# Merging an attention stream and a projection stream on one core: values one head behind, four shared PSUM banks, column tiles, gate products apart from the convolution

## The chip, the core and the metric

The kernel runs on one core of a Trainium2 chip. The metric is device time in microseconds (us). The names used below are those of the profile: PE is the matrix engine, PEld its weight loads, DVE the vector engine, ACT the scalar engine, POOL the general-purpose engine, SP the queue that issues most DMAs. PSUM is PE's output memory; the kernel's pools divide it into eight banks, and a tile of up to 512 fp32 columns takes one.

## The reference, cut to what matters

Two stages. The first is attention with a hash mask, over 4 batches of 8 heads (768 positions, 64 columns a head). The second is a gated long convolution on the attention's output, 512 columns wide.

```python
q_bits = (q @ proj > 0); k_bits = (k @ proj > 0)      # 6 bits each
mask = bucket(q_bits)[:, None] == bucket(k_bits)[None, :]
attn = softmax(where(mask, q @ k.T / 8, -1e9))         # per head
x = attn @ v                                           # heads side by side: 768 x 512
x1, x2, x3 = split(x @ w_proj, 3)
x2_conv = irfft(rfft(x2) * rfft(filter))               # along the sequence
out = (x1 * x2_conv * x3) @ w_out
```

## The kernel before

Heads are processed in pairs, 16 pairs in all, four pairs to a batch. For each pair the kernel transposes q and k on PE (`tps`), copies them out of PSUM with a scale on DVE (`tz`), multiplies by the hash matrix in fp32 on PE (`zps`), and makes +-0.5 bits on DVE that become extra rows of the operands (`pr_q`, `pr_k`). Scores (`stp`) go to exp on ACT (`pt`), and values (`pv`) follow. ACT copies one half of `pv` to `S`, and DVE adds it to the other half, which gives `T`. The normalisation goes through memory: row sums leave by DMA (`lt`), a reciprocal (`rl`), out to DRAM (`rdr`) and back, spread over the partitions (`R`). `U` multiplies by R, and `xh` and `xl` are its fp16 high and low halves. The projection of a batch then has x2 (`x2a`, `x2b`, `x2c`), a transform by matrices (`fdft`, with `u` and `z` on DVE), its inverse (`ida`, `idrq`, giving `cv`), x1 and x3 (`x`, 384 columns), and `wout`.

```python
psS = tile_pool(bufs=2)      # scores: 2 banks each
psV = tile_pool(bufs=1)      # values: 2 banks
psW = tile_pool(bufs=2)      # all the rest: 1 bank each

def prep(g, which):          # ... transposes into tps, tz ...
    for hf in range(2):
        zps = psW.tile([70, HALF], ...)
        nc.tensor.matmul(zps, projpad, tz[:, cs])       # fp32, 70 weight columns
        nc.vector.tensor_scalar(row[(which, 0)][64:70, cs], zps[64:70, :], ...)
        nc.vector.tensor_scalar(row[(which, 1)][0:6, cs], zps[0:6, :], ...)

def head(g, par, vpr, S, T):
    for jt in range(NCH):                               # 6 chunks
        stp = psS.tile([P, SEQ], ...)                   # two matmuls, 512 + 256
        nc.scalar.activation(pt[:, 0:SEQ], stp, AF.Exp, ...)
    pv = psV.tile([P, SEQ + 1], ...)
    for jt in range(NCH): ...                           # two matmuls each, 512 + 257
    nc.scalar.copy(S[rows, :], pv[HD:P, :])
    nc.vector.scalar_tensor_tensor(T[rows, :], in0=S[rows, :], ..., in1=pv[0:HD, :])

def pair(g):                 # ... both heads ...
    nc.sync.dma_start(lt[:, par, :], S[r0 : r0 + 1, 0:SEQ])
    # ... rl = 1 / (lt + eps); rdr <- rl; R <- rdr ...
    nc.vector.scalar_tensor_tensor(U, in0=T[:, 0:SEQ], scalar=vsd, op0=ALU.add, in1=R, op1=ALU.mult)
    # ... xh = fp16(U) on DVE, xl = U - xh on POOL ...

for b in range(1, NBAT):
    for pr in range(NPAIR):
        pair(b * NPAIR + pr); prep_pair(b * NPAIR + pr + 2)
    phase_b(b - 1, fbp)      # the whole projection of the batch before
phase_b(NBAT - 1, fbp)
```

A recording layer takes these instructions and orders them on each engine before the kernel runs, by its own model of when each is ready. At run time each engine's order is fixed.

The softmax here doesn't subtract the row's maximum and nothing guards it: scores larger than these inputs give would overflow.

Of the kernel before, what the change touches and what calls it, by code (L numbers as in the profile page):

```python
# [15 lines left out]
P = 128  # L16
SEQ = 768
# [69 lines left out]
def kernel(  # L87
# [35 lines left out]

    cp = ctx.enter_context(tc.tile_pool(name="consts", bufs=1))
    drp = ctx.enter_context(tc.tile_pool(name="drs", bufs=2, space=bass.MemoryType.DRAM))
    psS = ctx.enter_context(tc.tile_pool(name="psS", bufs=2, space=bass.MemoryType.PSUM))
    psV = ctx.enter_context(tc.tile_pool(name="psV", bufs=1, space=bass.MemoryType.PSUM))
    psW = ctx.enter_context(tc.tile_pool(name="psW", bufs=2, space=bass.MemoryType.PSUM))
    natp = ctx.enter_context(tc.tile_pool(name="nat", bufs=5))
    tzp = ctx.enter_context(tc.tile_pool(name="tz", bufs=2))  # L130
# [4 lines left out]
    nc.sync.dma_start(cst_sb, cst_d.ap())  # L135
    ident = cst_sb[:, 0:P]
    mask = cst_sb[:, P : P + 1]
    projpad = cp.tile([P, 70], FP32, name="projpad")
    nc.vector.memset(projpad, 0.0)
    nc.sync.dma_start(projpad[0:HD, 64:70], proj)  # L140
    nc.sync.dma_start(projpad[HD:P, 0:6], proj)
# [15 lines left out]
    PW = SEQ + 4  # L157
    pts = []
    for i in range(NPT):
        t_ = cp.tile([P, PW], FP16, name=f"pt_{i}")  # L160
        nc.gpsimd.memset(t_[:, SEQ : SEQ + 1], 1.0)
        pts.append(t_)
    pt_next = [0]
    vts = []
    for i in range(2):
        pv_ = []
        for par in range(2):
            t_ = cp.tile([P, NCH, P], FP16, name=f"vt_{i}_{par}")
            nc.gpsimd.memset(t_[:, :, LROW : LROW + 1], 1.0)
            pv_.append(t_)  # L170
        vts.append(pv_)

    def nat_load(src, b, pr, which):

        shape = [P, 2, 3, 2, HD] if which == "v" else [P, 3, 2, 2, HD]
        t_ = natp.tile(shape, FP32, tag="nat", name=f"nat_{which}")
        for par in range(2):
            head = src[b, 2 * pr + par].rearrange("(c p j) d -> p c j d", c=3, p=P, j=2)
            if which == "v":
                nc.sync.dma_start(t_[:, par], head)  # L180
            else:
                for j in range(2):
                    nc.sync.dma_start(t_[:, :, j, par, :], head[:, :, j, :])
        return t_

    def prep(g, which):
        b, pr = divmod(g, NPAIR)
        nat = nat_load(q if which == "q" else k, b, pr, which)
        row = prs[g % NPR]
        tz = tzp.tile([P, SEQ], FP32, tag="tz", name="tz")  # L190
        scl = QSCL if which == "q" else KSCL
        for hf in range(2):
            cs = slice(HALF * hf, HALF * hf + HALF)
            tps = psW.tile([P, HALF], FP32, tag="w", name=f"tps_{which}")
            for i in range(3):
                c3, j = divmod(3 * hf + i, 2)
                nc.tensor.transpose(  # L197
                    tps[:, ts(i, P)], nat[:, c3, j].rearrange("p h d -> p (h d)"), ident
                )
            nc.vector.tensor_scalar(tz[:, cs], tps, scl, None, ALU.mult)  # L200
        nc.gpsimd.tensor_copy(row[(which, 0)][0:HD, :], tz[0:HD, :])
        nc.gpsimd.tensor_copy(row[(which, 1)][HD:P, :], tz[HD:P, :])
        for hf in range(2):
            cs = slice(HALF * hf, HALF * hf + HALF)
            zps = psW.tile([70, HALF], FP32, tag="w", name=f"zps_{which}")
            nc.tensor.matmul(zps, projpad, tz[:, cs])  # L206
            nc.vector.tensor_scalar(
                row[(which, 0)][64:70, cs], zps[64:70, :], 0.0, 0.5, ALU.is_gt, ALU.subtract
            )
            nc.vector.tensor_scalar(  # L210
                row[(which, 1)][0:6, cs], zps[0:6, :], 0.0, 0.5, ALU.is_gt, ALU.subtract
            )

    def v_prep(g):
        b, pr = divmod(g, NPAIR)
        nat = nat_load(v, b, pr, "v")
        vs = []
        for par in range(2):
# [9 lines left out]
            vs.append(vpr)  # L228
        return vs

    KR = {0: slice(0, 70), 1: slice(0, P)}

    def head(g, par, vpr, S, T):
        row = prs[g % NPR]
        qp, kp = row[("q", par)], row[("k", par)]
        kr = KR[par]
        pl = []
        for jt in range(NCH):
            stp = psS.tile([P, SEQ], FP32, tag="s", name="stp")
            for lo_c, hi_c in ((0, 512), (512, SEQ)):  # L240
                nc.tensor.matmul(  # L241
                    stp[:, lo_c:hi_c], kp[kr, ts(jt, P)], qp[kr, lo_c:hi_c]
                )
            pt = pts[pt_next[0] % NPT]
            pt_next[0] += 1
            nc.scalar.activation(pt[:, 0:SEQ], stp, AF.Exp, bias=nmatch, scale=LSCALE)  # L246
            pl.append(pt)
        pv = psV.tile([P, SEQ + 1], FP32, tag="pv", name="pv")
        for jt in range(NCH):
            for lo_c, hi_c in ((0, 512), (512, SEQ + 1)):  # L250
                nc.tensor.matmul(  # L251
                    pv[:, lo_c:hi_c], vpr[:, jt, :], pl[jt][:, lo_c:hi_c],
                    start=(jt == 0), stop=(jt == NCH - 1),
                )
        rows = slice(HD * par, HD * par + HD)
        nc.scalar.copy(S[rows, :], pv[HD:P, :])  # L256
        nc.vector.scalar_tensor_tensor(  # L257
            T[rows, :], in0=S[rows, :], scalar=mask[rows, :], op0=ALU.mult,
            in1=pv[0:HD, :], op1=ALU.add,
        )  # L260

    xh = {}
    xl = {}

    def pair(g):
        b, pr = divmod(g, NPAIR)
        vs = v_prep(g)
        S = nrm.tile([P, SEQ + 1], FP32, tag="S", name="S")
        T = nrm.tile([P, SEQ + 1], FP32, tag="T", name="T")
        for par in range(2):  # L270
            head(g, par, vs[par], S, T)
# [25 lines left out]

    tabs = {}
# [13 lines left out]
    def setup(stg):  # L312
# [46 lines left out]
        for jp in range(3):  # L359
            ab = []  # L360
            for zone in range(2):
# [5 lines left out]
                for i, (lh, rh) in enumerate(terms):  # L367
                    nc.tensor.matmul(ps, lh, rh, start=(i == 0), stop=(i == len(terms) - 1))
                wc = cst_sb[:, P + 1 + jp : P + 2 + jp]
# [32 lines left out]
    def group(dest, terms):  # L402
        for i, (lh, rh) in enumerate(terms):
            nc.tensor.matmul(dest, lh, rh, start=(i == 0), stop=(i == len(terms) - 1))  # L404

    def phase_b(b, fbp):
        xhb = [xh[(b, f)] for f in range(NF)]
        xlb = [xl[(b, f)] for f in range(NF)]

# [9 lines left out]
        for j in range(2):  # L419
            ps = psW.tile([P, DM], FP32, tag="w", name="x2a")  # L420
            group(ps, x2_terms(2 + j))
            x1s = fbp.tile([P, DM], FP32, tag="x1s", name="x1s", bufs=1)
            nc.scalar.copy(x1s, ps)
            ps = psW.tile([P, DM], FP32, tag="w", name="x2b")
            group(ps, x2_terms(4 + j))
# [4 lines left out]
            ps = psW.tile([P, DM], FP32, tag="w", name="x2c")  # L430
            group(ps, x2_terms(j))
            s_, p_ = fold(ps, e_, j, fbp, 1)
            sj.append(s_)
# [3 lines left out]
        for jp in range(3):  # L437
            us = {}
            for zone in range(2):
                ps = psW.tile([P, DM], FP32, tag="w", name="fdft")  # L440
                group(ps, [(hi, rhs) for hi, _, rhs in fwd_terms(jp, zone, sj, pj, dj)])
                for o, hm in enumerate(((hA, hB), (hB, hD))[zone]):
                    u_ = fbp.tile([P, DM], FP32, tag=f"u{zone}{o}", name="u_", bufs=1)
                    nc.vector.tensor_tensor(u_, ps, hm[jp], ALU.mult)
                    us[(zone, o)] = u_
            for o in range(2):
# [5 lines left out]
        yT = []  # L452
        for ct in range(NF):
            cc = ts(ct, P)
            pa = psW.tile([P, T3], FP32, tag="w", name="ida")
            group(pa, [(Z[i][:, cc], tabs["ia"][:, i, :]) for i in range(2)])
            asb = fbp.tile([P, T3], FP32, tag="asb", name="asb")
            nc.scalar.copy(asb, pa)  # L458
            prq = psW.tile([P, 2 * T3], FP32, tag="w", name="idrq")
            group(prq, [(Z[2 + i][:, cc], tabs["irq"][:, i, :]) for i in range(4)])  # L460
            cv = fbp.tile([P, SEQ], FP32, tag="cv", name="cv", bufs=1)
            nc.vector.tensor_tensor(cv[:, 0:T3], asb, prq[:, 0:T3], ALU.add)
            w_ = fbp.tile([P, T3], FP32, tag="w_", name="w_")
# [7 lines left out]
            y_ = fbp.tile([P, SEQ], FP16, tag=f"y{ct}", name="y_", bufs=1)  # L471
            for hf in range(2):
                cs = slice(HALF * hf, HALF * hf + HALF)
                for nt in (ct, 2 * NF + ct):
                    px = psW.tile([P, HALF], FP32, tag="w", name="x13")
                    t_ = []
                    for f in range(NF):
                        st_h = wph[f][:, ts(nt, P)]
                        t_.append((st_h, xhb[f][:, cs]))
                        t_.append((st_h, xlb[f][:, cs]))  # L480
                        t_.append((wpl[f][:, ts(nt, P)], xhb[f][:, cs]))
                    group(px, t_)
                    if nt == ct:
                        m_ = fbp.tile([P, HALF], FP32, tag="m_", name="m_")
                        nc.vector.tensor_tensor(m_, cv[:, cs], px, ALU.mult)
                    else:
                        nc.vector.scalar_tensor_tensor(
# [69 lines left out]
```

## Time and profile before

| | before |
|---|---|
| median (first 3 runs) | 559.93 us (557.51 to 561.39) |
| PE, DVE, ACT, POOL busy | 89%, 57%, 38%, 27% |
| matmul floor from start-to-start medians | 459 us |
| of the span not covered by it | 102 us |

The page of the kernel before: busy time and number of instructions of each engine, then three of the slice rows, in which each digit is the busy tenths of a fortieth of the span (PEclk is the granted clock in tenths).

```profile
PE 500.9 (89%) x2552; PEld 258.7 (46%) x2552; DVE 318.5 (57%) x567; ACT 213.2 (38%) x273; POOL 153.1 (27%) x206
...
PE   5988379998989999999988999999995999977997
...
DVE  4779876775763854437762954447349433166430
...
PEclk9999688998989999999989999999999999999999
```

PE is nearly always busy from slice 6 on, and its low digits are at the start, in slices 4 and 5, counted from 0 (set-up of the convolution's tables), at slice 30 (the last batch waits for its own normalisation) and, less, at slices 35 and 36. PE's busy time counts the pipeline's ends, so the floor of 459 us is the better measure of what PE needs: it is the usual distance from one matmul's start to the next, times the count.

Two rows of the waits of the kernel before (who waited for whom: us in total, times, longest):

```profile
DVE U L289 <- DMA R<-rdr: 24.0, 11, 6.1
...
PE pv L251 <- POOL vt_0_131 L225: 8.0, 1, 8.0
```

The hash matmuls in the groups of the kernel before (line, engine, operation, tiles, shapes, count, then busy us and mean ns, then the idle time before them):

```profile
L206 PE MATMUL zps_k<-tz,projpad 128*70 128x384 f32 x64 | 28.9, 562 | 0.0
...
L206 PE MATMUL zps_q<-tz,projpad 128*70 128x384 f32 x64 | 27.3, 524 | 1.6 <-DVE tz L200 1.6
```

Each fp32 matmul leaves two records, 0.323 us from start to start, so the 128 records need 41.3 us of PE.

Stages of the kernel before, as windows (us from the start; then busy us of each engine with its count, the granted clock, DMA share and GB/s):

```profile
0.00:113.00 113.00, 87.85 (x399) 44.19 (x400) 84.39 (x134) 56.93 (x68) 69.38 (x97) 0.92 0.60 165
113.00:410.00 297.00, 280.88 (x1467) 147.21 (x1465) 169.56 (x312) 143.57 (x183) 80.45 (x108) 0.98 0.23 59
```

The columns after the length are PE, PEld, DVE, ACT and POOL.

### The profile page before, as it was taken

Reading aid. Unit: us, or ns where it says so; the run is one execution under the profiler, and the core shown is the slowest. Engines: PE = TensorE matmul, PEld = TensorE weight load, DVE = VectorE, ACT = ScalarE, POOL = GpSimd, SP = SyncE. Lnnn points to the kernel's source line nnn. Section 1 sums busy time; section 2 is a strip of 40 time slices with the busy share of each in tenths; the row PEclk is TensorE's granted clock in tenths of the full one; section 3 lists DMA queues with packets and bytes.
Section 4 is the critical chain, followed back from the end, with each engine's and each line's share of the span. In section 5 each row is a group of like instructions: output and inputs, shape, how many; then the busy total and the mean of one; then the engine's idle time right before and its main releaser. Section 6 shows DMA issues by size and latency. Waiting matters only on the chain.

```text
span 561.3 us, 7069 instructions
## 1 busy us (share of the span) xinstructions
PE 500.9 (89%) x2552; PEld 258.7 (46%) x2552; DVE 318.5 (57%) x567; ACT 213.2 (38%) x273; POOL 153.1 (27%) x206
## 2 busy tenths in 40 slices
PE   5988379998989999999988999999995999977997
PEld 2454134454434455545443455544442555434553
DVE  4779876775763854437762954447349433166430
ACT  0677224886852612037861612047920001200002
POOL 1656974664551101115651101124111000000000
PEclk9999688998989999999989999999999999999999
DMA  6686724634432001044432001020010000200002
GB/s 150 170 288 185 211 66 103 150 90 103 108 96 60 0 1 29 30 140 117 101 97 57 0 2 42 16 112 27 20 41 1 1 1 19 95 1 1 0 2 112
DMA packets 82084, 39.93 MB, mean 71 GB/s; under 512 B 61953, under 2 KB 74753, under 8 KB 82049
## 3 DMA queue, kind: packets, MB, share of 16 engines
q1 hardware_dynamic: 82048, 39.48, 25.5%
q8 instruction: 20, 0.33, 0.2%
q14 instruction: 16, 0.12, 0.1%
HBM read 32.97 MB, written 6.39 MB: 70 GB/s over the span
## 4 chain that ended last, share of the span: by engine, by line
PE 64%; DVE 12%; DMA 9%; ACT 7%; issue 3%; POOL 3%; SPq 2%; DVEq 0%; ACTq 0%; POOLq 0%
PE wout L404 7%; PE pv L251 6%; PE stp L241 5%; DMA R<-rdr 4%; DMA rdr<-rl 3%; PE zps_k L206 3%; PE x2a L404 3%; PE x2c L404 3%; PE x2b L404 3%; PE zps_q L206 3%; PE idrq L404 3%; PE fdft L404 2%; PE tps_k L197 2%; ACT S L256 1%; POOL xl L295 1%
## 5 line engine op out<-in xcount | busy, mean ns | idle before, releaser
L458 ACT COPY asb<-ida 128x256 f32<-128x256 f32 x16 | 6.0, 373 | 136.5 <-PE ida L404 136.5
L295 POOL TENSOR_TENSOR xl<-U,xh 128x768 f16<-128x768 f32 x16 | 28.5, 1779 | 100.5 <-DVE xh L293 98.1
L256 ACT COPY S<-pv 64x769 f32<-64x769 f32 x32 | 25.5, 798 | 48.1 <-PE pv L251 47.9
L257 DVE SCALAR_TENSOR_TENSOR T<-S,cst_sb,pv 64x769 f32<-64x769 f32 x32 | 32.3, 1010 | 17.6 <-ACT S L256 17.1
L501 ACT ACTIVATE osb<-wout 128x512 f32<-128x512 f32 x24 | 14.3, 598 | 65.6 <-PE wout L404 65.6
L200 DVE TENSOR_SCALAR tz<-tps_q 128x384 f32<-128x384 f32 x32 | 17.0, 549 | 33.3 <-PE tps_q L197 29.3
L289 DVE SCALAR_TENSOR_TENSOR U<-T,vsd,R 128x768 f32<-128x768 f32 x16 | 16.3, 1017 | 24.0 <-DMA R<-rdr 24.0
L404 PEld LDWEIGHTS <-xh 128*128 128x128 f16 x192 | 18.8, 98 | 22.2 <-issue 0.2
L206 PE MATMUL zps_k<-tz,projpad 128*70 128x384 f32 x64 | 28.9, 562 | 0.0
L206 PE MATMUL zps_q<-tz,projpad 128*70 128x384 f32 x64 | 27.3, 524 | 1.6 <-DVE tz L200 1.6
L197 PE MATMUL tps_k<-cst_sb,nat_k 128*128 128x128 f32 x96 | 18.1, 301 | 8.5 <-DVE pr_q_1_96 L210 4.4
L197 PE MATMUL tps_q<-cst_sb,nat_q 128*128 128x128 f32 x96 | 17.3, 290 | 9.4 <-DMA nat_q<-in_q_dram 6.5
L241 PE MATMUL stp<-pr_q_0_89,pr_k_0_92 70*128 70x512 f16 x72 | 19.1, 351 | 2.0 <-ACT pt_129 L246 0.8
L246 ACT ACTIVATE pt_107<-stp,nmatch 128x768 f16<-128x768 f32 x16 | 14.4, 901 | 15.4 <-PE stp L241 15.2
L221 POOL CAST vt_1_133<-nat_v 128x384 f16<-128x384 f32 x8 | 4.0, 504 | 58.5 <-PE pv L251 54.2
L246 ACT ACTIVATE pt_117<-stp,nmatch 128x768 f16<-128x768 f32 x16 | 14.4, 900 | 14.2 <-PE stp L241 14.2
L197 PEld LDWEIGHTS tps_k<-cst_sb,nat_k 128*128 128x128 f32 x96 | 11.2, 149 | 18.3 <-issue 9.4
L246 ACT ACTIVATE pt_111<-stp,nmatch 128x768 f16<-128x768 f32 x16 | 14.4, 901 | 12.0 <-PE stp L241 11.7
L197 PEld LDWEIGHTS tps_q<-cst_sb,nat_q 128*128 128x128 f32 x96 | 11.9, 147 | 14.9 <-issue 6.7
L200 DVE TENSOR_SCALAR tz<-tps_k 128x384 f32<-128x384 f32 x32 | 17.4, 543 | 2.4 <-PE tps_k L197 2.1
L241 PE MATMUL stp<-pr_q_0_90,pr_k_0_93 128*128 128x512 f16 x72 | 16.9, 325 | 1.9 <-ACT pt_123 L246 1.0
L246 ACT ACTIVATE pt_113<-stp,nmatch 128x768 f16<-128x768 f32 x16 | 14.4, 900 | 10.6 <-PE stp L241 10.6
(1284 smaller groups left out, 1387.3 us busy)
## 6 DMA issues: line engine op xcount, KB each, us to landing
nat_q<-in_q_dram SPq DMA_DIRECT2D x64, 96.0 KB, 2.6
nat_k<-in_k_dram SPq DMA_DIRECT2D x64, 96.0 KB, 2.5
nat_v<-in_v_dram SPq DMA_DIRECT2D x32, 192.0 KB, 3.7
R<-rdr SPq DMA_DIRECT2D x32, 192.0 KB, 3.5
out_dram<-osb SPq DMA_DIRECT2D x24, 256.0 KB, 2.0
o_622<-in_moe_w_out_dram SPq DMA_DIRECT2D x1, 1024.0 KB, 7.5
flt_578<-in_moe_filter_fft_dram SPq DMA_DIRECT2D x1, 768.0 KB, 5.4
flt_588<-in_moe_filter_fft_dram SPq DMA_DIRECT2D x1, 768.0 KB, 5.0
```

The lines of the kernel that those rows point to most:

```text
L197: nc.tensor.transpose(tps[:, ts(i, P)], nat[:, c3, j].rearrange("p h d -> p (h d)"), ident)
L200: nc.vector.tensor_scalar(tz[:, cs], tps, scl, None, ALU.mult)
L206: nc.tensor.matmul(zps, projpad, tz[:, cs])
L241: nc.tensor.matmul(stp[:, lo_c:hi_c], kp[kr, ts(jt, P)], qp[kr, lo_c:hi_c])
L246: nc.scalar.activation(pt[:, 0:SEQ], stp, AF.Exp, bias=nmatch, scale=LSCALE)
L251: nc.tensor.matmul(pv[:, lo_c:hi_c], vpr[:, jt, :], pl[jt][:, lo_c:hi_c], start=(jt == 0), stop=(jt == NCH - 1),)
L256: nc.scalar.copy(S[rows, :], pv[HD:P, :])
L257: nc.vector.scalar_tensor_tensor(T[rows, :], in0=S[rows, :], scalar=mask[rows, :], op0=ALU.mult, in1=pv[0:HD, :], op1=ALU.add,)
L289: nc.vector.scalar_tensor_tensor(U, in0=T[:, 0:SEQ], scalar=vsd, op0=ALU.add, in1=R, op1=ALU.mult)
L295: nc.gpsimd.tensor_tensor(tl, U, th, ALU.subtract)
L404: nc.tensor.matmul(dest, lh, rh, start=(i == 0), stop=(i == len(terms) - 1))
L501: nc.scalar.mul(osb, po, 1.0 / YSCALE)
```

## The change

Its intent: PE is the limit but has holes, so give it something else to do in each of them. Five things change at once.

1. Both streams become generators that hand out one matmul at a time, and a loop merges them: about 400 ns of projection for 300 ns of attention, starting after 5.2 pairs.
2. A head's values are taken while the next head's scores are made.
3. The values' own two banks and the two work banks become four shared single banks, with the values in two pieces of 512 and 257 columns.
4. The hash of q and of k are put into different column ranges of PE, side by side.
5. For half of the column tiles, x1*x3 is made ahead, between the `fdft` groups, in place of waiting for the convolution.

Smaller parts go with them: in the last batch's projection every third PSUM tile comes from the score banks, the set-up's matmuls are handed out between steps of attention, some loads use another queue, and some buffer counts differ.

```diff
-    psV = ...tile_pool(name="psV", bufs=1, space=PSUM)
-    psW = ...tile_pool(name="psW", bufs=2, space=PSUM)
+    psW = ...tile_pool(name="psW", bufs=4, space=PSUM)
...
-            zps = psW.tile([70, HALF], FP32, tag="w", name=f"zps_{which}")
-            nc.tensor.matmul(zps, projpad, tz[:, cs])
+            zps = psW.tile([P, HALF], FP32, tag="w", name="zps")
+            for i in (1, 0):                                  # k, then q
+                mm = nc.tensor.matmul(zps[64 * i : 64 * i + 38, :], projpad, tzs[i][:, cs])
+                # ... ordered after the one before (manual edge) ...
...
+    def pv_gen(g, par, pl):
+        for lo_c, hi_c in ((0, 512), (512, SEQ + 1)):
+            pv = psW.tile([P, hi_c - lo_c], FP32, tag="w", name="pv")
+            for jt in range(NCH):
+                nc.tensor.matmul(pv, vpr[:, jt, :], pl[jt][:, lo_c:hi_c], ...)
+                if jt == NCH - 1:      # S, T of this piece; after the last: finish(g)
+                    ...
+                yield (hi_c - lo_c) * 0.42
...
+                for jt in range(NCH):                         # in attn_gen
+                    # ... scores, exp ...
+                    for half in range(2):
+                        yield pv.take(200 if jt < 3 else 100) # values of the head before
+                        # ... some of the transposes of a later pair ...
+                pv = Feed(pv_gen(g, par, pl))
...
+        yield from gate_gen(0, 0)                             # x1*x3 ahead
+        yield from fdft_gen(0)
+        yield from gate_gen(0, 1)
+        yield from fdft_gen(1)
...
+    for b in range(NBAT):
+        pg = Feed(proj_gen(b, fbp, b == NBAT - 1))
+        while pg.live:
+            t_ = attn.take(300)
+            owed += (t_ or 300) * PROJ_NS / (4 * PAIR_NS)
+            owed -= pg.take(owed)
```

`finish(g)`, with the DMAs of the normalisation and `U`, is as before; it is only called from another place. The constants and the first loads of k go through ACT's DMA queue.

## The prediction

> **What bounds the kernel now.** TensorE, with holes. Busy table: PE 500.9 us of a 561.3 us span (89%), DVE 57%, ACT 38%; the chain of waits is 64% PE. Busy time overstates the need: start-to-start medians of consecutive matmuls in the trace times their counts (512 columns 0.216 us, 384 columns 0.163, 257 columns 0.110, fp32 transpose 0.110, zps record 0.323) give a floor of 459 us: scores 62, values 63, transposes 21, zps 41, setup 9, projection 66 per batch. About 102 us are holes, by the timeline: 6 before the first matmul, 9 until 31 us, 25 in 31-99 us (setup; one 8.0 us PE wait on POOL vt; clock 0.87), 17 in 99-169 us (attention alone), 3-9 in each later stage, 8.5 at 421-440 us (last normalisation, DMA rdr and R), 6 at 500-515 us (fdft waiting for DVE u), 3.5 after the last matmul.
>
> **What the change does.**
> 1. Projection of a batch is spread over the next four pairs' attention, from pair 5.2 on, and values run one head behind scores, so a PE wait on exp, DVE, POOL or the normalisation has other matmuls to fill it. Attention alone is ACT-paced: 12 exps of 0.90 us plus S copies make 12.5 us per pair, PE needs 11.7.
> 2. The last batch no longer waits for its normalisation (-8); gate products between fdft groups hide the DVE u/z chain (-5 twice).
> 3. zps of q and k go side by side in column tiles. The Trainium skill ("TensorE: Matmul & The Clock Gate", Part 3) says column tiles overlap and matmuls start in order. Each zps has two records of 0.323 us; in the order k, q, k, q with overlap between neighbours only, 5 slots replace 8: 41 to about 27 us. No trace here shows it yet.
> 4. Added: S and T in two pieces, about +0.2 us per head on ACT and DVE, and 16 ACT copies of about 0.48; off the critical path except early.
>
> **Sum.** Until pair 5.2 I expect DVE to bind: setup 27 us (casts, wpl, folds, h), prep 6.6 us a pair for 7.2 pairs, the rest 4.7 a pair for 4.5 pairs: 95 us after 7 us of start, so about 100 us. The rest of PE's new floor of 445 us, about 377 us, runs 96-97% dense: 388. Tail 3.5. With rounding down for early overlap, about **488 us**, 80% range **467 to 513**. Chances: faster by over 2% 0.95, within 2% 0.04, slower 0.01.
>
> **What would show each step right or wrong.** zps records start to start: below 0.25 us on average, total about 27 us; wrong if still 41. Slices: PE 9 from about slice 8 to the end, clock 1.0 there. Waits of PE: POOL vt gone, fdft on DVE u below 2 us in total, few waits for a PSUM bank (four shared). DVE above 85% busy in the first 100 us; the first x2a matmul at about 100 us.
>
> **What would make it wrong.** A values group holds one of four shared banks most of the time: the projection may stall on evacuation (510 or more). POOL beside DVE in setup (one subtraction took 4.9 us) could hold vt and the row copies. If DVE does not bind early, the first stage ends near 82 us and the total falls to 470. PE is in order: one matmul merged ahead of its late input blocks both streams.

## The result, and the profile after

The changed kernel takes 523.37 us (median of 4 runs, 519.18 to 524.05) against 560.38 us of the kernel before on the same chip. Ratios in this document are the mean time of one kernel's runs over the mean of the other's in the same rounds, so they are not quite the ratio of the medians quoted; here it is 0.933 (95% interval 0.927 to 0.939). The change is faster, but the predicted 488 us and its range up to 513 us were missed.

The page of the changed kernel, the same rows:

```profile
PE 469.4 (90%) x2552; PEld 248.6 (48%) x2552; DVE 322.5 (62%) x591; ACT 229.8 (44%) x321; POOL 156.1 (30%) x206
...
PE   4797657988998989999898998989999999999997
...
DVE  4888987893756887353747878463645783036830
...
PEclk9898869998998999999999999999999999999999
```

The end is dense now (nothing but 9 from slice 27, at 352 us, to the last slice but one), so the hole at the last batch is gone. The start is hardly better: slices 3 to 6 still show 7, 6, 5 and 7. The middle has a sprinkling of eights that the prediction didn't expect.

The stages of the changed kernel, with the window edges as before:

```profile
0.00:113.00 113.00, 83.93 (x413) 40.66 (x414) 89.54 (x146) 61.05 (x80) 71.76 (x98) 0.91 0.63 162
113.00:410.00 297.00, 279.01 (x1558) 150.93 (x1557) 180.03 (x344) 153.68 (x213) 81.16 (x108) 0.99 0.23 60
```

In the first 113 us PE starts 413 matmuls, 14 more than before. The first projection matmul, expected at about 100 us, starts at 113.7 us.

The waits of DVE and PE in the changed kernel:

```profile
DVE T L276 <- ACT S L275: 57.3, 28, 5.5
DVE U L304 <- DMA R<-rdr: 20.5, 12, 3.1
...
PE tps_q L198 <- DVE T L276: 6.6, 2, 5.2
PE zps L215 <- DVE tz L202: 5.6, 4, 2.5
...
PE zps L215 <- DVE fd L524: 2.5, 1, 2.5
...
PE x_1677 L488 <- DVE u__1653 L569: 2.1, 1, 2.1
...
PE wout L488 <- DVE tz L202: 1.8, 1, 1.8
```

PE's wait for POOL's `vt` is gone, as expected. `U` still holds DVE for 20.5 us. And PE waits for DVE in places where the two instructions have no data in common: `tps_q` doesn't read T, `zps` doesn't read fd, `wout` doesn't read tz. In these rows the matmul needs a PSUM bank that the DVE instruction was the last to read (`zps` on `tz` is an ordinary wait for data). DVE's largest wait is that of `T` for ACT's copy `S`, 57.3 us; no run moved `T`, and the wait stays at 51.8 us in the kernel with late U below, so it is not what that kernel gains.

One such case, DVE's timeline around 250 us in the changed kernel (start, us, instruction, and in brackets the idle time before it with what ended it):

```profile
250.36 1.02 DVE L304 SCALAR_TENSOR_TENSOR U<-T,vsd,R 128x768 f32<-128x768 f32 x1 [3.13 <-DMA R<-rdr]
251.30 0.68 DVE L522 TENSOR_TENSOR e__2526<-x1s,x2b 128x512 f32<-128x512 f32 x1
251.89 0.55 DVE L308 CAST xh<-U 128x768 f16<-128x768 f32 x1
252.36 0.68 DVE L524 TENSOR_TENSOR fd<-x1s,x2b 128x512 f16<-128x512 f32 x1
252.96 0.55 DVE L202 TENSOR_SCALAR tz<-tps_k 128x384 f32<-128x384 f32 x1
```

And PE's timeline in the same stretch:

```profile
248.03 0.38 PE L488 MATMUL x2b<-wpl_614,xh 128*128 128x512 f16 x1
...
250.20 0.38 PE L488 MATMUL x2c<-wpl_602,xh 128*128 128x512 f16 x1
253.10 1.17 PE L215 MATMUL zps<-tz,projpad 128*38 128x384 f32 x6 [2.52 <-DVE fd L524]
```

The x2b product is complete at 248.4 us. Its readers `e_` and `fd` (sum and difference with `x1s`, which ACT had copied by 245.1) could run then; DVE is idle. But they stand behind `U`, which waits for its DMA until 250.36. PE gets its bank at 253.1. One late DMA has held DVE for 3.1 us and PE for 2.5 us, and DVE had work that was ready. The Trainium skill says so of the queues ("TensorE: Matmul & The Clock Gate", table at the top): PE's may pull weight loads ahead, the other three engines' are strict first in, first out. This trace agrees for DVE.

The hash in the changed kernel's groups:

```profile
L215 PE MATMUL zps<-tz,projpad 128*38 128x384 f32 x128 | 29.0, 561 | 8.1 <-DVE tz L202 5.6
```

In an undisturbed block (282.8 us) the records of the two tiles start in twos, 7 ns apart, and two twos take 0.345 and 0.42 us: 0.78 us per half where four records before took 1.29. The start-to-start sum of all records, with the cold ones, went from 49.5 to 28.1 us.

### The profile page after: what moved, and what is told of

It is laid out like the page before. It is cut to its first block, busy times and chain, and to the rows that moved or that the text cites. A ratio compares the mean times of both kernels' runs of the same rounds, so it can differ in the third digit from the quotient of the medians.

```text
span 521.2 us, 7013 instructions
## 1 busy us (share of the span) xinstructions
PE 469.4 (90%) x2552; PEld 248.6 (48%) x2552; DVE 322.5 (62%) x591; ACT 229.8 (44%) x321; POOL 156.1 (30%) x206
## 4 chain that ended last, share of the span: by engine, by line
PE 50%; DMA 17%; DVE 16%; issue 7%; POOL 5%; SPq 3%; ACT 2%; DVEq 0%; ACTq 0%; POOLq 0%
PE wout L488 8%; DMA R<-rdr 7%; PE pv L270 5%; DMA rdr<-rl 5%; PE stp L354 4%; PE x2b L488 3%; PE x2c L488 3%; PE zps L215 3%; PE x2a L488 2%; PE idrq L488 2%; DMA nat_v<-in_v_dram 2%; SPq L177 2%; PE fdft L488 2%; DVE U L304 1%; DMA flt_572<-in_moe_filter_fft_dram 1%
## 5 line engine op out<-in xcount | busy, mean ns | idle before, releaser
L276 DVE SCALAR_TENSOR_TENSOR T<-S,cst_sb,pv 64x512 f32<-64x512 f32 x64 | 38.9, 608 | 58.0 <-ACT S L275 57.3
L310 POOL TENSOR_TENSOR xl<-U,xh 128x768 f16<-128x768 f32 x16 | 26.5, 1654 | 97.0 <-DVE xh L308 97.0
L275 ACT COPY S<-pv 64x512 f32<-64x512 f32 x64 | 30.5, 477 | 46.1 <-PE pv L270 30.4
L215 PE MATMUL zps<-tz,projpad 128*38 128x384 f32 x128 | 29.0, 561 | 8.1 <-DVE tz L202 5.6
L198 PE MATMUL tps_q<-cst_sb,nat_q 128*128 128x128 f32 x96 | 24.9, 297 | 11.1 <-DVE T L276 6.6
L198 PE MATMUL tps_k<-cst_sb,nat_k 128*128 128x128 f32 x96 | 24.7, 288 | 7.7 <-DMA nat_k<-in_k_dram 2.5
L304 DVE SCALAR_TENSOR_TENSOR U<-T,vsd,R 128x768 f32<-128x768 f32 x16 | 16.5, 1032 | 23.5 <-DMA R<-rdr 20.5
L198 PEld LDWEIGHTS tps_q<-cst_sb,nat_q 128*128 128x128 f32 x96 | 13.8, 151 | 20.4 <-DVE T L276 7.4
L359 ACT ACTIVATE pt_115<-stp,nmatch 128x768 f16<-128x768 f32 x16 | 14.5, 904 | 16.8 <-PE stp L354 16.6
L359 ACT ACTIVATE pt_111<-stp,nmatch 128x768 f16<-128x768 f32 x16 | 14.4, 901 | 15.5 <-PE stp L354 15.5
L198 PEld LDWEIGHTS tps_k<-cst_sb,nat_k 128*128 128x128 f32 x96 | 13.4, 147 | 16.4 <-issue 4.3
L359 ACT ACTIVATE pt_112<-stp,nmatch 128x768 f16<-128x768 f32 x16 | 14.4, 903 | 15.4 <-PE stp L354 15.2
L359 ACT ACTIVATE pt_106<-stp,nmatch 128x768 f16<-128x768 f32 x16 | 14.4, 902 | 14.9 <-PE stp L354 14.9
L359 ACT ACTIVATE pt_104<-stp,nmatch 128x768 f16<-128x768 f32 x16 | 14.4, 901 | 14.2 <-PE stp L354 7.3
L359 ACT ACTIVATE pt_110<-stp,nmatch 128x768 f16<-128x768 f32 x16 | 14.4, 902 | 11.8 <-PE pv L270 6.3
L488 PEld LDWEIGHTS <-wph_594 128*128 128x128 f16 x128 | 12.3, 98 | 13.8 <-issue 4.8
```

The lines of the kernel that those rows point to most:

```text
L198: nc.tensor.transpose(tps[:, ts(i, P)], nat[:, c3, j].rearrange("p h d -> p (h d)"), ident)
L215: mm = nc.tensor.matmul(zps[64 * i : 64 * i + 38, :], projpad, tzs[i][:, cs])
L275: nc.scalar.copy(S[rows, lo_c:hi_c], pv[HD:P, :])
L276: nc.vector.scalar_tensor_tensor(T[rows, lo_c:hi_c], in0=S[rows, lo_c:hi_c], scalar=mask[rows, :], op0=ALU.mult, in1=pv[0:HD, :], op1=ALU.add,
L310: nc.gpsimd.tensor_tensor(tl, U, th, ALU.subtract)
L359: nc.scalar.activation(pt[:, 0:SEQ], stp, AF.Exp, bias=nmatch, scale=LSCALE)
```

## The experiments

Seventeen kernels were run, in five groups. "Gain" in the text is a difference of ratios times 560 us. All are correct except one.

| run | what it is | median us | ratio to before (interval) |
|---|---|---|---|
| (the change) | | 523.4 | 0.933 (0.927 to 0.939) |
| late_u | change, U one head later on DVE | 505.7 | 0.898 (0.892 to 0.904) |
| spread_setup | change, set-up spread out | 525.6 | 0.935 (0.928 to 0.942) |
| three_banks | change, three shared banks | 549.7 | 0.974 (0.967 to 0.982) |
| zps_full | change, hash not side by side | 539.2 | 0.959 (0.952 to 0.965) |
| no_gate | change, gates undone | 525.6 | 0.940 (0.934 to 0.946) |
| no_lag | change, values behind own scores | 525.3 | 0.939 (0.932 to 0.947) |
| no_merge | change, merge undone | 523.2 | 0.934 (0.930 to 0.939) |
| no_order | change, the three above undone together | 538.1 | 0.957 (0.952 to 0.961) |
| late_u_act_casts | late_u, weight casts on ACT | **495.4** | 0.885 (0.880 to 0.890) |
| late_u_tiny_bits | late_u, hash bits cut (wrong result) | 495.0 | 0.884 (0.878 to 0.890) |
| relief | late_u_act_casts, still more on ACT | 501.8 | 0.895 (0.891 to 0.899) |
| late_u_three_banks | late_u, three banks | 526.8 | 0.940 (0.936 to 0.945) |
| late_u_casts_no_merge | late_u_act_casts, merge undone | 510.8 | 0.907 (0.903 to 0.912) |
| late_u_casts_spread | late_u_act_casts, set-up spread out | 497.7 | 0.883 (0.880 to 0.887) |
| before_late_u | before, U one head later | 557.5 | 0.994 (0.990 to 0.998) |
| before_banks | before, four shared banks | 557.5 | 0.989 (0.984 to 0.994) |
| before_banks_zps | before, banks and column tiles | 542.1 | 0.962 (0.958 to 0.966) |

The theory after the first look (Q): DVE is a queue, U stands at its head waiting for R, and the bank that PE wants stands behind U. Its rivals: DVE simply has too much work (L), and four shared banks are too few (B).

### Moving U in the queue

```diff
                     if par == 1 and lo_c:
                         finish(g)                 # now ends after the DMAs of R
+                    if par == 0 and lo_c and g > 0:
+                        finish_late(g - 1)        # vsd, U, xh, xl
...
+        tc.add_manual_dep(um.ins, lastT[0].ins.name, ...)   # U behind the next head's T
```

The work is the same; only U's place in DVE's order changes. The manual edge is needed: without it the recording layer put U back into the place it had, by the author's reading because in its own model R has landed by then (seen in the built order; no run shows it).

> The changed kernel, with the normalising product U (and xh, xl behind it) ordered after the next head's last T on DVE, about one head later; same work. Theory Q (DVE is a queue: U stands at its head waiting for the DMA of R, 20.5 us in all, and what PE needs stands behind it): DVE's idle time before U for R falls from 20.5 to under 4 us, PE's lost time between 113 and 410 us falls from about 30 to about 15 us, and the time falls from 523 to about 505-512 us. Rival L (DVE simply has too much work in the merged stages, 76% busy in 100-200 us): no change beyond 3 us. Rival B (four PSUM banks are too few): no change either.

Measured: 505.7 us, a gain of 20 us over the change. The wait in the kernel with late U, a little over the 4 us that were expected at most:

```profile
DVE U L314 <- DMA R<-rdr: 4.4, 3, 2.1
```

Its stages:

```profile
0.00:113.00 113.00, 87.56 (x420) 42.32 (x421) 89.18 (x148) 62.47 (x81) 72.08 (x100) 0.89 0.64 164
113.00:410.00 297.00, 289.96 (x1644) 158.19 (x1643) 196.21 (x373) 155.54 (x217) 84.87 (x107) 1.00 0.24 61
```

Between 113 and 410 us PE now starts 1644 matmuls where the change starts 1558, and DVE does 196.2 us of work there where it did 180.0. DVE wasn't short of capacity in the merged stages; it was held. Theory Q stands for them, and L falls there; so does B as the only cause. Nothing changes in the first 113 us beyond 7 matmuls. The first x2a in the changed kernel and, below it, in the one with late U:

```profile
113.67 0.38 PE L488 MATMUL x2a<-wph_594,xh 128*128 128x512 f16 x1
```

```profile
112.33 0.38 PE L508 MATMUL x2a<-wph,xh 128*128 128x512 f16 x1
```

From there to the end of the span the change takes 407.5 us (of 521.2) and the kernel with late U 391.1 (of 503.4). The prediction had 388 and a tail of 3.5. With U out of the way, the merged stages are as dense as predicted.

The same edit on the kernel before (there `lt`, `rdr` and `R` stay in place and U follows the next head's T):

> The kernel before the change, with U ordered after the next head's T on DVE and nothing else. It has the same wait (24.0 us of DVE idle before U for R). If that wait already cost the kernel before: 545-552 in place of about 560. If only the finer merge is exposed to it (before, PE's holes have other causes, coarse projection pieces stand between): within 5 us of 560.

It brings 0.6%, about 3 us, though U's wait for R falls from 24.0 to 9.6 us:

```profile
DVE U L299 <- DMA R<-rdr: 9.6, 8, 2.3
```

The wait was there before the change, and taking 14 us of it away gained little; taking 16 us of it away in the changed kernel gained 20. Which part of the change made the wait expensive was not tested.

### The first stage

The spread-out set-up only adds yields between weight blocks:

```diff
             wpl.append(tl)
+            yield 1500.0
...
             wol.append(tl2)
+            yield 600.0
```

> The changed kernel, with the setup's casts and subtractions given out one weight block at a time between attention steps up to about pair 5, in place of all at once after pair 2. Theory Q (the lump stands in the DVE and POOL queues ahead of what attention needs: one pair took 38 us there): the fifth pair's scores start at about 88 us in place of 97, the first x2a at about 105 us in place of 114, the time falls by 6-10 us. Rival L (the sum of DVE work up to pair 5.2 sets the stage, about 90 us of it): the first x2a stays at 111-116 us and the time within 3 us.

Nothing: 525.6 us, the first x2a at 116.0. The theory that the lump's place in the queues matters (called Q here too) falls. The next two runs change how much DVE has to do there.

```diff
-            nc.vector.tensor_copy(th, w32)         # four of these, 1536 columns
+            nc.scalar.copy(th, w32)
...
-            nc.vector.tensor_copy(th2, o32[:, c, :])
+            nc.scalar.copy(th2, o32[:, c, :])
```

> The late-U kernel with the eight casts of the projection weights (about 11 us of DVE in the changed kernel, stretched where POOL subtracts beside them) moved from DVE to ACT, which is nearly idle then. Theory L for the first stage (the sum of DVE work up to pair 5.2, with POOL beside it, sets it): the first x2a at about 102-106 us in place of 112, and 496-501 us in place of 505.7. If the first stage waits for something else (DMA, order): 503-507.

```diff
-   row[(which, par)][r0 : r0 + 6, cs], zs[hf][z0 : z0 + 6, :],
+   row[(which, par)][r0 : r0 + 6, cs.start : cs.start + 8], zs[hf][z0 : z0 + 6, 0:8],
```

> The late-U kernel with the 128 hash-bit comparisons on DVE cut from 384 columns to 8 (result wrong on purpose): about 60 of DVE's 322 us gone, no instruction less. Theory L for the first stage: the first x2a at about 98-103 us, total about 488-495. If DVE's load no longer matters once U is out of the way: 502 or more. Later stages have little left to gain (PE lost about 10 us between 113 and 410 us in the late-U kernel).

Both gain 0.013 to 0.014 of the ratio, about 8 us (the medians say 10), over late_u. The first x2a moves from 112.3 us to 102.0 and to 105.7; in the kernel with the casts on ACT:

```profile
102.03 0.38 PE L508 MATMUL x2a<-wph,xh 128*128 128x512 f16 x1
```

The second expectation, 98 to 103, was missed. So DVE's work counts in the first stage, but not one for one: up to the first x2a the casts take DVE's busy time from 89 to 79 us and the stage gets 10 us shorter, the bits take it from 89 to 70 us and the stage gets only 7 us shorter. DVE is not full there either: it is busy 78.6 of the first 100 us in the changed kernel. So it binds only in part. The PSUM banks and the lag also move the first x2a (see below). Part of DVE's busy time is stretched work. DVE and POOL in the changed kernel:

```profile
51.79 0.41 DVE L435 CAST woh_618<-o_616 128x512 f16<-128x512 f32 x1
52.00 4.36 POOL L429 TENSOR_TENSOR wpl_596<-w_592,wph_594 128x1536 f16<-128x1536 f32 x1 [5.42 <-DVE wph_594 L426]
52.13 0.41 DVE L435 CAST woh_622<-o_616 128x512 f16<-128x512 f32 x1
52.46 0.94 DVE L426 CAST wph_600<-w_598 128x1536 f16<-128x1536 f32 x1
53.33 3.31 DVE L435 CAST woh_626<-o_616 128x512 f16<-128x512 f32 x1
```

The same cast takes 0.41 us twice and 3.31 us the third time; then it ends just after POOL's subtraction does. The two casts between, which also start inside POOL's recorded span, are not stretched (the one of 1536 columns took 0.94 us before POOL started, too). But POOL's subtraction itself takes 4.36 us, where the same one takes 3.10 us at 63.1 us in the kernel with the casts on ACT. It looks as if POOL waited for these casts and then held the next one; that order is inferred. The Trainium skill ("SBUF — State Buffer", Who interferes with whom) describes a pair of memory ports that DVE and POOL share, which copies and casts on DVE can take and for which one of the two blocks for a whole instruction. This trace agrees with it. How much of the gain comes from the contention, and how much from the work moved, was not told apart.

Moving still more to ACT (the filter's scalings and half of the transposes' evacuation):

```diff
-  nc.vector.tensor_scalar(tA, ps, wc, None, ALU.mult)
+  nc.scalar.mul(tA, ps, wc)                       # and tB
...
+  if which == "k":
+      nc.scalar.mul(tz[:, cs], tps, scl)
```

> A candidate: the kernel with late U and the weight casts on ACT, and besides it the six filter scalings and the k half of the transposes' evacuation on ACT: about 22 us more of DVE's work moved (17.5 tz, 4.4 filter). By theory L of the first stage, the first x2a moves from 102 to about 95-98 us and the time from 495.4 to 486-492. If ACT, which paces attention with 12.5 us a pair, has become the limit (it gets about 14 us in the first stage): 494 or more.

It was 501.8 us, slower than without. The first x2a moves back to 108.6 us. DVE's wait for the hash and PE's wait for exp in that kernel and, below it, in the one with the casts alone:

```profile
DVE pr_q L235 <- PE zps L218: 27.3, 13, 7.6
...
PE stp L374 <- ACT pt L379: 8.2, 12, 3.7
```

```profile
DVE pr_q L232 <- PE zps L215: 9.0, 11, 3.2
...
PE stp L371 <- ACT pt L376: 4.2, 9, 1.0
```

DVE had 11 us less to do in the first 113 us and it didn't help. The expectation's second branch came true. That ACT has become the limit fits PE's longer wait for exp; but the hash is also late, whose input `tz` now stands in ACT's queue. Which of the two costs the 6 us was not tested.

Spreading the set-up once the casts are gone:

> The kernel with late U and the casts on ACT (495.4), with the setup given out block by block up to about pair 5. Alone, on the changed kernel, that did nothing (525.6 against 523.4). If the lump counts once the load is relieved: 486-491. If not: 493-498.

497.7 us, ratio 0.883 against 0.885: the same.

### The banks

```diff
-    psW = ...tile_pool(name="psW", bufs=4, ...)
+    psW = ...tile_pool(name="psW", bufs=3, ...)
```

> The changed kernel with three shared PSUM banks in place of four. Rival B (banks are what the merged stages lack): over 20 us longer, 545 us or more. Theories Q and L (the bank waits only pass on a late DVE): 3 to 12 us longer.

> The late-U kernel with three shared PSUM banks. Three banks cost the changed kernel 26 us. If banks were short because DVE, held at U, released them late, three banks cost the late-U kernel (505.7) clearly less: 515-522. If the bank count counts by itself: 528 or more.

One bank fewer costs 23 us in the changed kernel (0.041) and 24 us with late U (0.042), where U's wait stays short (3.1 us); 526.8 us lies between the two branches expected. Half of it is lost before the first x2a, which moves from 113.7 to 126.2 us, and with late U from 112.3 to 124.3. So the banks count apart from U, and the bank count is as large a term. Theory B expected the time of the first run, but no change from late U, and there it was wrong. Whether a fifth bank would shorten the first stage stays open: none was tried, since the two score tiles hold the other four.

### The column tiles

```diff
-    mm = nc.tensor.matmul(zps[64 * i : 64 * i + 38, :], projpad, tzs[i][:, cs])
+    mm = nc.tensor.matmul(zps, projpads[i], tzs[i][:, cs], start=(i == 1), stop=(i == 0))
```

Here both hash matmuls use the full width and add into one bank, with zero weights where the other has its columns, so that they cannot run side by side.

> The changed kernel with the hash projection of q and of k as two full-width matmuls that add into one bank (weights zero elsewhere) in place of column tiles side by side; the result is right. It sizes step 3 of the prediction: the zps records' start-to-start sum goes from 28 to about 42-45 us and the time is 11 to 16 us longer, because PE is the limit in most stages. If PE were not the limit where the hash is computed, under 6 us.

The records' start-to-start sum is 45.9 us, and the time rises by 0.026, about 14 us. The prediction's 14 us for this step was right.

### Where the rest of the gain comes from

The first three undo one part each:

```diff
 # no_gate: fdft groups together; then inverse, x1, x3 for each column tile
-        yield from gate_gen(0, 0)
-        yield from fdft_gen(0)
...
+        for jp in range(3):
+            yield from fdft_gen(jp)
 # no_lag: values taken right behind the head's own scores
-                while pv.live:
-                    yield pv.take(200)
                 pv = Feed(pv_gen(g, par, pl))
+                while pv.live:
+                    yield pv.take(200)
 # no_merge: four pairs of attention, then one batch's projection
-            t_ = attn.take(300)
+            t_ = attn.take(4 * PAIR_NS)
+            pg.drain()
```

> The changed kernel with the gate products undone: fdft groups stand together, then each column tile's inverse, x1 and x3 as before the change, still merged with attention. It sizes step 2 of the prediction. If the merge hides the DVE u/z chain in the first batches by itself, only the last two batches (whose projection runs mostly without attention) pay some 5-6 us each: 8 to 14 us longer than the changed kernel (523). If the gates matter in every batch: 20 us or more. If they do nothing: within 4 us.

> The changed kernel with each head's values right behind its own scores in place of one head later; merge, banks and tiles as changed. If the lag is what keeps ACT's exps going (attention alone needs 12.5 us a pair on ACT) and PE off the last exp of each head: 15 to 30 us longer, most of it before the first x2a. Rival: the recording layer reorders by readiness anyway and fills the place, so under 6 us.

> The changed kernel with the merge of attention and projection undone in the program order: four pairs of attention, then one batch's projection in one piece; lag, banks, column tiles and gates stay. It sizes step 1. If the merge is where the gain comes from: 535 or more, near zps and banks apart. Rival: the recording layer already interleaves ready matmuls by its own model, so the order in the program matters little: 518-528.

No single one costs more than 0.7%, and their intervals overlap the change's. Undoing the merge costs nothing at all, although its order is truly different (the first x2a at 167.9 us in place of 113.7). The lag does the opposite of what was expected in the first stage: undone, the first x2a starts at 106.7 us, earlier than with it (113.7; 406 matmuls come before it in place of 416), and the gain is lost again later. Going the other way, from the kernel before:

> The kernel before with one part of the change: the values' two-bank tile and the two work banks become four shared single banks, values in two pieces (512 and 257 columns). If shared banks are the main gain besides the column tiles (39 - 16 = 23 us left): 536-545 in place of 560. If the banks only count together with the merged order: 555 or more.

> The kernel before with four shared banks and the hash in column tiles side by side; order, lag and gates as before. If these two parts are the whole gain: 519-528, as the changed kernel (523). If the merged order gives some by itself: 532 or more.

The edit of the first replaces `psV` and `psW` by four shared banks and splits the values into two pieces; the second adds the side-by-side hash as in the change. Banks give 6 us and the tiles 15 us more; 16 us of the change's gain are missing (0.962 against 0.933). Then all three orders were undone together:

> The changed kernel (523) with merge, lag and gates all three undone in the program order; banks, column tiles and the two load queues stay. Each alone cost 0 to 2 us. If they stand in for one another (each fills the same PE holes), all three together cost what banks and tiles alone leave: 536-545, as the kernel before with banks and tiles (542). If none is worth anything: 521-529, and the 19 us come from something not named yet.

538.1 us, 0.957: undone together they cost 13 us, give or take 4, undone one at a time 1 to 4 and 8 in all, give or take 12 (by the medians 15 us together and 4 in all). This fits parts that stand in for one another: each gives PE something ready to do in the same holes, so each seems worthless while the others are there. But by the ratios the difference is not clear of noise, so it is suggested and not shown. The remaining 3 us (0.957 against 0.962) lie within the intervals.

The last question was whether the merge is worth something once DVE is no longer held:

> The kernel with late U and the casts on ACT (495.4), with the program order's merge undone as before (four pairs, then one batch's projection). If the merge is worth its 15-25 us only once DVE no longer holds PE: 508-520. If the recording layer's order makes it worthless anyway: 492-499.

It is: 0.907 against 0.885, 13 us. But this run doesn't isolate the filling of holes. Without the merge a head is shorter, the next head's T comes too soon for R, and U holds DVE again for 16.5 us (with the merge and the casts 3.8):

```profile
DVE U L314 <- DMA R<-rdr: 16.5, 10, 3.3
```

So the merge may pay partly by giving the DMA its time. How much each part is, stays open.

## Why the prediction was right or wrong

**The sum.** Predicted 488 us, measured 523.4. In the prediction's own terms the profiled run (523.0) lost 14 us in the first stage (113.7 for 100) and 16 us in the rest with its tail (407.5 for 388 + 3.5). The other 5 are the 3.5 that the prediction rounded down and 1.8 outside the profiled span. The mechanism of a denser PE was right, and the kernel that has it, with U late and the casts on ACT, takes 495.4. Two terms of the sum were mis-sized, and the two corrections recover 27 of the 35 us (by ratios).

- *"The rest of PE's new floor ... runs 96-97% dense: 388."* This is the step that failed most. From the first x2a (113.7 us) to the end it took 407 us for about 376 us of matmuls (start-to-start times, as in the floor), 92%. The reason given for the density, "a PE wait on exp, DVE, POOL or the normalisation has other matmuls to fill it", is false for DVE: PE's order is fixed and DVE's order is fixed, and a U that waits up to 3.1 us for R holds the banks that PE needs next. With U moved, a gain of 20 us, PE runs 1644 matmuls in the window where the change ran 1558, and the rest takes 391.1 us, 96%. The prediction had seen 24.0 us of that wait in the profile before only as a hole at the last batch, and had counted it as removed.
- *"Until pair 5.2 I expect DVE to bind ... about 100 us."* DVE did bind in part, but the stage took 113.7 us. The work was not underestimated: 95 us expected, 90 us busy up to the first x2a, although one cast was stretched eightfold beside POOL. The step that failed is that DVE would run through it at 95%. It ran at 79% in the first 100 us, against the stated 85% or more. Moving 11 us of casts off DVE brought the first x2a from 112.3 to 102.0 us; cutting the comparisons, 19 us up to there, brought it only to 105.7. What DVE waits for in its idle fifth was not isolated; the bank count and the lag move this stage as well.
- What is left, 495 against 488, is nearly all arithmetic: in the profiled run with late U and the casts on ACT (495.5 us) the first stage is 102.0 us for 100 and the rest 391.7 for 391.5, and the 3.5 rounded down and 1.8 outside the span come on top. The first stage could perhaps be shorter still. The first scores start at 17.2 us in the changed kernel, 15.6 before, with PE waiting for the first loads of k from ACT's queue (landing after 4.1 us, against 2.6 from SP). No run tested that.

**zps.** Right in size (14 us by undoing it), not quite in mechanism: the pairs overlap wholly, four slots and not five of eight, and a change of tiling costs on each side of a block, so that the sums come out alike.

**The last normalisation and the gates.** The hole at the last batch is gone, as predicted (the score banks that its projection now shares may help; not tested). "-5 twice" for the gates was too much: undoing them alone costs at most 4 us, an amount that the intervals don't set apart from zero.

**"few waits for a PSUM bank".** Wrong. The bank waits are PE's typical waits in the profile after, and one bank fewer costs 23 us. The warning that the projection "may stall on evacuation" named what happens, without its cause: the DVE instruction that frees the bank stands behind U.

**Step 1, merge and lag.** The prediction made them the main gain. Banks and column tiles give 21 of the change's 37 us (by ratio), which leaves 16 for merge, lag, gates and the smaller parts. Undone together the three cost 13 us; none alone costs an amount that is clear of noise.

## What to carry to other kernels

When an engine is the limit and its order is fixed, giving it more ready work doesn't help against a wait at the head of another engine's queue: look for the instruction that idles its engine until a DMA lands, and move that instruction back in the order until the DMA has had its time. Test a bundle of changes both ways, by undoing one part and by adding one part, since parts that fill the same holes can look worthless one at a time. And don't take the sum of an engine's work for the length of a stage: here 90 us of DVE's work filled 113.7 us, and part of it was stretched by the neighbour on its memory ports.

## What the Trainium skill lacked or had wrong

- "TensorE: Matmul & The Clock Gate", Part 3, gives overlap of column tiles (its picture, of row tiles, has them start about 4 ns apart) but no figure for fp32. Two fp32 tiles of 38 columns overlap here too: their records start 6 to 7 ns apart, and 0.78 us replace 1.29 us per half.
- "TensorEngine Tiling (Array Packing)", Key Properties, says that changing the tiling mode drains the engine, without a figure. Here the last records of a tiled block take 0.42 us where the ones before them take 0.345, and a 256-column matmul ahead of a block 0.20 us in place of 0.11: some 0.07 to 0.09 us each way. With full-width hash matmuls (zps_full) the last records of a block take 0.32 us like the others.
- "SBUF — State Buffer", Who interferes with whom, tells of the shared ports and of the factor for single instructions, but not what they cost a stage in which both engines cast and subtract. Here a 128x512 cast went from 0.41 to 3.31 us and a subtraction on POOL from 3.10 to 4.36 us; what the stage lost by it was not measured.
- No page that was read has the cost of the whole chain of a normalisation that goes out to DRAM and back: issue to landing takes 2.1 us (row sums), 2.7 us (reciprocals out) and 3.6 us (back, spread over the partitions), median, and it is this that held DVE.
- "PSUM — Partial Sum Buffer" says to evacuate promptly, without what a bank is worth: with two streams on four shared banks, one bank fewer cost 23 us of 523.
